# Decode holds the magnitude at a least value, GpSimd leaves the arithmetic, first pp w_in is one float32 product, w_out follows w_in

## The chip, the cores and the metric

The kernel runs on 1 core of one Trainium2 chip. Its engines are TensorE (PE in the profile, with PEld for the loads of the stationary operand), VectorE (DVE), ScalarE (ACT), GpSimd (POOL) and SyncE (SP), whose queue issues every DMA here. The metric is the device time in microseconds (us). Before the change the median of 3 runs is 1566.36 us (1564.33 to 1568.11).

## The reference, cut to what matters

```
p_packed = softmax(scale * p @ k.T) @ v            # attn1: 32 rows of p per head, 576 keys
x        = softmax(scale * q @ p_packed.T) @ p_packed   # attn2, reshaped to 4608 x 512
h = x @ w_in ;  r = maximum(h, 0)
g = s * (r * r) + b ;  x2 = g @ w_out              # 512 -> 2048 -> 512
a = x2 @ w1 ;  bb = x2 @ w2
out = ((a * bb) @ w3) @ w_out2                     # 512 -> 1024 -> 1024 -> 512
```

Batch 8, 8 heads, 576 tokens each, head width 64. All tensors are float32 in the reference; the weights reach the kernel as 64-bit floats.

## The kernel before, in words

A weight tile is loaded as 128 x 512 64-bit floats (512 KB) and turned into 32-bit floats by bit work (class `Decode`): `square` (L147, ACT) makes a mask tile `m`, `bits1` and `bits2` (L151, L157, L164, DVE) shift and join the two halves of each number, and a last step multiplies by the mask, either on DVE (L169) or in two GpSimd operations (L173, L176). `raw` holds three loads at a time, `x` three decoded tiles.

Products run as three float32r matmuls: `mm3` (L87, L90, L91) multiplies a high and a low part, which `split` makes (L80 or L82 the high part, L84 the low part, DVE or GpSimd).

The order of the work is one Python program; a scheduler turns it into one fixed order for each engine and for the DMA queue of SP. It runs in these stages:

- Start. `attn1_steps(0, ...)` computes the packed p of batches 0 and 1 (units u = 0 to 3), and beside it the 16 tiles of w_in are decoded into `winx`. Then `attn2_steps(0)` computes the attention of batch 0; beside it `W_split` and `W_tile` fold packed p into w_in: 16 products of a w_in tile (`wps`), whose results are split into `wph`, `wpl` for batch 0 and stored as `w2_d` for batch 1. After them `win_store` (L578) writes the 16 decoded tiles to DRAM.
- Steady part. 256 steps, 32 for a batch: `step_h(idx+2)` makes h (6 matmuls), `r` (ACT, L641), `g` (DVE, L643), and its two halves `gh` (ACT, L80) and `gl` (GpSimd, L84); `step_x(idx)` multiplies them by w_out tile f = idx mod 16 (12 matmuls into four banks). After each 16 steps `xst` (L675, L677) takes the result. In the first 16 steps `wo_load` and `wo_dec` load and decode one tile of w_out each. Beside the steps run: attn2 of the next batch, attn1 of the next pair of batches, the W tiles for that pair (steps 49, 113 and 177 on; w_in is loaded again and split each time), and from step 36 on `job`, which decodes the weights of the second part. The last 8 pairs of jobs (step 144 on) end in `combine`: seven sums of w1 and w2 are split into one buffer `Shl` and stored (L715).
- Second part: products with w1, w2 (`prod`), then with w3 and w_out2 (`yps`). The change touches nothing there but the name of a buffer.

Of the kernel before, what the change touches and what calls it, by code (L numbers as in the profile page):

```python
# [22 lines left out]
def fused_kernel(  # L23
# [51 lines left out]
    TINY = 1.125 * 2.0 ** -30  # L75
# [22 lines left out]
    win_d = [tc.dram_tile([P, FC], F32, name=f"win_{n}") for n in range(NFC * NPAIR)]  # L98
    x2_d = [[tc.dram_tile([DM, HS], F32, name=f"x2_{b}_{h}") for h in range(2)] for b in range(B)]
# [26 lines left out]
    RAWB, XB = 3, 3  # L126
# [4 lines left out]
    class Decode:  # L131
# [13 lines left out]
        def square(self):  # L145
            self.m = dec.tile([P, 512], BF16, tag="m", name="m", bufs=2)
            nc.scalar.activation(self.m, self.hf, AF.Square)  # L147

        def bits1(self, pin=False, out=None):
            self.x = dec.tile([P, 512], I32, tag="x", name="x", bufs=XB) if out is None else out  # L150
            ins = nc.vector.tensor_scalar(  # L151
                out=self.x, in0=self.hw, scalar1=3, scalar2=0x3FFFFFFF,
                op0=ALU.logical_shift_left, op1=ALU.bitwise_and,
            )
            if pin:
                tc.keep_in_program_order(ins)
            nc.vector.scalar_tensor_tensor(  # L157
                out=self.x, in0=self.hw, scalar=-0x40000000, in1=self.x,
                op0=ALU.bitwise_and, op1=ALU.bitwise_or,
            )  # L160

        def bits2(self, e2="v"):
            xu, xf = self.x.bitcast(U32), self.x.bitcast(F32)
# [4 lines left out]
            if e2 == "v":  # L168
                nc.vector.scalar_tensor_tensor(  # L169
                    out=xf, in0=self.m, scalar=TINY, in1=xf, op0=ALU.is_ge, op1=ALU.mult  # L170
                )
            else:
                nc.gpsimd.tensor_scalar(  # L173
                    out=self.m, in0=self.m, scalar1=TINY, scalar2=None, op0=ALU.is_ge
                )
                nc.gpsimd.tensor_tensor(out=xf, in0=self.m, in1=xf, op=ALU.mult)  # L176
            self.f = xf

    if True:
# [28 lines left out]
        def q_sc(b, t, ps):  # L208
            for pr in range(NPAIR):
                c = 64 * (pr ^ (b % 2))  # L210
                for o in range(tok(t) // SUB):
# [3 lines left out]
                        ppT[b // 2][:, pr, b % 2, :], start=True, stop=True,  # L215
# [193 lines left out]
        def D_ev(u, ps_of):  # L409
            b, g = divmod(u, NG)  # L410
            if u % 4 == 0:
                ppT[b // 2] = ppp.tile([P, NPAIR, 2, 2 * NP], F32, tag="ppT", name="ppT", bufs=2)
# [3 lines left out]
                ppT[b // 2][:, 2 * g:2 * g + 2, b % 2, :],  # L416
# [6 lines left out]
        def pp_split(bp):  # L423

            hi = stg.tile([P, NPAIR, P], F32R, tag="pph", name="pph", bufs=1)
            lo = stg.tile([P, NPAIR, P], F32R, tag="ppl", name="ppl", bufs=1)
            for o in range(2):
                for bb in range(2):
                    c = slice(64 * (bb ^ o), 64 * ((bb ^ o) + 1))
                    split(hi[:, o::2, c], lo[:, o::2, c], ppT[bp][:, o::2, bb, :])  # L430
# [44 lines left out]
        wd, wx = {}, {}  # L475

        def win_load(n):
            fc, pr = divmod(n, NPAIR)
            wd[n] = Decode(w_in[pr * P:(pr + 1) * P, fc * FC:(fc + 1) * FC])
# [4 lines left out]
        wo_t, wod = {}, {}  # L484

        def wo_load(f):
            wod[f] = Decode(w_out[f * P:(f + 1) * P, :], pin=f > 1)

        def wo_dec(f):
            d = wod.pop(f)  # L490
            d.square()
            d.bits1()
            d.bits2("g" if f % 4 == 3 else "v")
            if f >= NW // 2:
# [585 lines left out]
```

## Time and profile before

| | |
|---|---|
| median of 3 runs | 1566.36 us |
| the profiled execution | 1571.24 us, its span 1569.5 us |
| mean granted TensorE clock | 0.962 of full speed |
| busy: PE, DVE, ACT, POOL | 1467.2, 959.7, 632.5, 423.5 us |
| start, to the end of step 16 | 0 to 198.8 us |
| steps 17 to 256 | 198.8 to 955 us |
| second part | 955 to 1569.5 us |

The busy time of an engine is the union of its instructions; matmuls are pipelined, so a PE that is shown as busy may still lose time between them. The end of each 16 steps can be read from the first `xst` copy.

### The profile page before, as it was taken

How to read it: one execution, taken by the hardware profiler on the slowest of the kernel's cores; microseconds unless marked ns; L12 is line 12 of the kernel's file. 1: busy time of each engine (PE TensorE's matmuls, PEld its weight loads, DVE VectorE, ACT ScalarE, POOL GpSimd, SP SyncE). 2: the span in 40 equal slices, each digit the busy share in tenths (PEclk: the TensorE clock that was granted, in tenths of full speed). 3: DMA queues.
4: the chain of work that ended last, by engine and by line, in shares of the span. 5: the costliest groups of instructions: out<-in, count | busy, mean ns of one | idle time of the engine just before them, and what ended most of it. 6: DMA issues, size and time to landing. Idle time of an engine off the chain costs nothing.

```text
span 1569.5 us, 26929 instructions
## 1 busy us (share of the span) xinstructions
PE 1467.2 (93%) x10136; PEld 1336.9 (85%) x10136; DVE 959.7 (61%) x1913; ACT 632.5 (40%) x1465; POOL 423.5 (27%) x418
## 2 busy tenths in 40 slices
PE   6677799999999999988789999999999999999998
PEld 3356699999999889878579998899999999999996
DVE  6985844674657566756666425457665575756552
ACT  3465454565544565544555434212121131212111
POOL 6763623553334442434453331000000000000000
PEclk7578999999999999999889999999999999999999
DMA  9738532544535544533655115345656474555541
GB/s 247 208 98 232 154 103 73 158 147 128 142 108 171 161 143 138 156 120 121 201 174 169 57 46 181 109 163 206 218 193 212 164 244 162 183 196 167 202 161 41
DMA packets 142899, 245.57 MB, mean 156 GB/s; under 512 B 52144, under 2 KB 103344, under 8 KB 136624
## 3 DMA queue, kind: packets, MB, share of 16 engines
q1 hardware_dynamic: 142768, 243.84, 49.8%
q8 instruction: 80, 1.31, 0.4%
q14 instruction: 51, 0.42, 0.1%
HBM read 191.37 MB, written 52.43 MB: 155 GB/s over the span
## 4 chain that ended last, share of the span: by engine, by line
PE 71%; DMA 13%; DVE 9%; ACT 2%; issue 2%; POOL 1%; SPq 0%; ACTq 0%; DVEq 0%; POOLq 0%
PE prod L90 7%; PE prod L87 7%; PE prod L91 7%; DMA whl<-Shl 6%; PE xps L90 6%; PE xps L87 6%; PE xps L91 6%; PE yps L90 4%; PE yps L91 4%; PE yps L87 4%; PE hps L87 3%; PE hps L90 3%; PE hps L91 3%; DMA raw<-in_moe_w_out_dram 2%; DMA x<-win 1%
## 5 line engine op out<-in xcount | busy, mean ns | idle before, releaser
L84 POOL TENSOR_TENSOR gl<-g,gh 128x288 fp32r<-128x288 f32 (+1 forms) x256 | 228.3, 893 | 398.5 <-ACT gh L80 380.9
L90 PE MATMUL xps<-gl,wo 128*128 128x288 f32 (+1 forms) x1024 | 302.2, 302 | 3.8 <-POOL gl L84 3.6
L91 PE MATMUL xps<-gh,wo 128*128 128x288 f32 (+1 forms) x1024 | 298.4, 299 | 0.0
L87 PE MATMUL xps<-gh,wo 128*128 128x288 f32 (+1 forms) x1024 | 266.1, 302 | 7.4 <-POOL wo L84 5.2
L643 DVE SCALAR_TENSOR_TENSOR g<-hps,sb_s,r 128x288 f32<-128x288 f32 x256 | 130.6, 513 | 163.8 <-ACT r L641 152.4
L87 PE MATMUL prod<-xc,whl 128*128 128x384 f32 x672 | 225.8, 336 | 2.4 <-DMA whl<-whl 2.4
L90 PE MATMUL prod<-xc,whl 128*128 128x384 f32 x672 | 226.4, 337 | 0.0
L91 PE MATMUL prod<-xc,whl 128*128 128x384 f32 x672 | 225.8, 336 | 0.0
L90 PEld LDWEIGHTS xps<-gl,wo 128*128 128x128 f32 x1024 | 194.7, 190 | 10.0 <-POOL gl L84 6.8
L91 PEld LDWEIGHTS xps<-gh,wo 128*128 128x128 f32 x1024 | 194.6, 190 | 2.4 <-issue 1.4
L87 PEld LDWEIGHTS xps<-gh,wo 128*128 128x128 f32 x1024 | 180.8, 191 | 13.9 <-POOL wo L84 6.7
L87 PE MATMUL hps<-ATh,wpl 128*128 128x288 f32 x512 | 159.0, 311 | 13.0 <-DVE wpl L84 6.3
L90 PE MATMUL hps<-ATl,wph 128*128 128x288 f32 x512 | 155.3, 303 | 0.0
L91 PE MATMUL hps<-ATh,wph 128*128 128x288 f32 x512 | 154.9, 303 | 0.0
L80 ACT CAST gh<-g 128x288 fp32r<-128x288 f32 (+1 forms) x256 | 110.2, 432 | 104.6 <-DVE g L643 92.3
L641 ACT ACTIVATE r<-hps 128x288 f32<-128x288 f32 x256 | 104.3, 409 | 93.0 <-PE hps L91 91.9
L87 PEld LDWEIGHTS prod<-xc,whl 128*128 128x128 f32 x672 | 126.7, 189 | 9.8 <-issue 2.7
L90 PEld LDWEIGHTS prod<-xc,whl 128*128 128x128 f32 x672 | 126.6, 188 | 7.9
L91 PEld LDWEIGHTS prod<-xc,whl 128*128 128x128 f32 x672 | 126.7, 189 | 0.1
L87 PEld LDWEIGHTS hps<-ATh,wpl 128*128 128x128 f32 x512 | 99.0, 194 | 21.1 <-DVE wpl L84 9.3
L90 PE MATMUL yps<-w,c 128*128 128x512 f32 x288 | 113.5, 394 | 0.0
L87 PE MATMUL yps<-w,c 128*128 128x512 f32 x288 | 112.4, 391 | 0.3 <-DVE c L84 0.3
(327 smaller groups left out, 2605.9 us busy)
## 6 DMA issues: line engine op xcount, KB each, us to landing
whl<-whl SPq DMA_DIRECT2D x48, 1792.0 KB, 7.3
raw<-in_moe_w_dram SPq DMA_DIRECT2D x32, 512.0 KB, 4.6
whl<-Shl SPq DMA_DIRECT2D x56, 256.0 KB, 2.5
raw<-in_moe_w_out_dram SPq DMA_DIRECT2D x24, 512.0 KB, 4.1
x<-win SPq DMA_DIRECT2D x48, 256.0 KB, 3.0
k<-in_k_dram SPq DMA_DIRECT2D x16, 576.0 KB, 6.6
v<-in_v_dram SPq DMA_DIRECT2D x16, 576.0 KB, 6.4
q<-in_q_dram SPq DMA_DIRECT2D x72, 128.0 KB, 3.2
```

The costliest lines, as they stand in the source:

```text
L80: nc.scalar.copy(hi, src)
L84: eng.tensor_tensor(out=lo, in0=src, in1=hi.bitcast(F32), op=ALU.subtract)
L87: ins = nc.tensor.matmul(ps, wl, xh, start=start, stop=False)
L90: nc.tensor.matmul(ps, wh, xl, start=False, stop=False)
L91: nc.tensor.matmul(ps, wh, xh, start=False, stop=stop)
L641: nc.scalar.activation(r_, ps[:, :HS], AF.Relu)
L643: nc.vector.scalar_tensor_tensor(out=g[:, :HS], in0=ps[:, :HS], scalar=sb_s[:, 0:1], in1=r_, op0=ALU.mult, op1=ALU.mult)
```

## The change

- `Decode` no longer makes a mask. ACT writes the magnitude of the high word (`Abs`), DVE holds it at a least value 2^-15, then come the same three bit operations, the first of them now in place on the magnitude. No operation of it is on GpSimd.
- Low parts (`gl`, `wo`) go to DVE, and `g` becomes a square on ACT; the factor s is applied with `xst`. The sums of `combine`, one copy of p and a 2-column copy stay on GpSimd.
- The W tiles of the first pair of batches multiply packed p by w_in directly, as one float32 matmul instead of three float32r ones; no `W_split` there. Packed p lies so that the tile needs no rearranging, and `pp_split` is one split.
- One list of 32 tiles, w_in then w_out, is loaded three ahead and decoded by `dec_next`: in each step of the first attn1, in every third step of the first attn2, and in the first steps. Each `win_store` follows its W tile.
- The second pair's W tiles split w_in and store the split tile (`wsp_d`); the two later pairs load that (512 KB) instead of splitting.
- W tiles start three steps later (`WR` 20), attn1 of the later pairs starts at steps 0, 40 and 104 with units 8 or 12 steps apart, and `Shl` has two buffers.

```diff
-        def square(self):
-            self.m = dec.tile([P, 512], BF16, tag="m", name="m", bufs=2)
-            nc.scalar.activation(self.m, self.hf, AF.Square)
         def bits1(self, pin=False, out=None):
-            ins = nc.vector.tensor_scalar(
-                out=self.x, in0=self.hw, scalar1=3, scalar2=0x3FFFFFFF,
-                op0=ALU.logical_shift_left, op1=ALU.bitwise_and,
-            )
+            xi, xf = self.x.bitcast(I32), self.x.bitcast(F32)
+            ins = nc.scalar.activation(xf, self.hf, AF.Abs)
+            nc.vector.tensor_scalar_max(xf, xf, LEAST)
...
+            nc.vector.tensor_scalar(
+                out=xi, in0=xi, scalar1=3, scalar2=0x3FFFFFFF,
+                op0=ALU.logical_shift_left, op1=ALU.bitwise_and,
+            )
...
-            if e2 == "v":
-                nc.vector.scalar_tensor_tensor(
-                    out=xf, in0=self.m, scalar=TINY, in1=xf, op0=ALU.is_ge, op1=ALU.mult
-                )
-            else:
-                nc.gpsimd.tensor_scalar(
-                    out=self.m, in0=self.m, scalar1=TINY, scalar2=None, op0=ALU.is_ge
-                )
-                nc.gpsimd.tensor_tensor(out=xf, in0=self.m, in1=xf, op=ALU.mult)
-            self.f = xf
+            self.f = self.x.bitcast(F32)
...
         def W_split(k, src):
-            hi = stg.tile([P, FC], F32R, tag="sh", name="sh", bufs=2)
-            lo = stg.tile([P, FC], F32R, tag="sl", name="sl", bufs=2)
-            split(hi, lo, src, "s" if k % 2 else "v", "g")
-            sw[k] = (hi, lo)
+            t = stg.tile([P, 2, FC], F32R, tag="shl", name="shl", bufs=WB)
+            split(t[:, 0], t[:, 1], src)
+            nc.sync.dma_start(out=wsp_d[k], in_=t.bitcast(F32))
+            sw[k] = t
...
-            ph, pl = pps[bp]
-            wh, wl = sw.pop(k)
-            mm3(ps, ph[:, pr, :], pl[:, pr, :], wh, wl, True, True)
+            if bp == 0:
+                nc.tensor.matmul(
+                    ps, ppT[0][:, 2 * pr:2 * pr + 2, :].rearrange("p a c -> p (a c)"), win_at(k),
+                    start=True, stop=True,
+                )
+            else:
+                ph, pl = pps[bp]
+                t = sw.pop(k)
+                mm3(ps, ph[:, pr, :], pl[:, pr, :], t[:, 0], t[:, 1], True, True)
...
+        def dec_next():
+            n = ndec[0]
+            if n >= NW + FB1:
+                return
+            ndec[0] += 1
+            d = dq.pop(0)
+            if n < NW:
+                d.bits1(out=win_at(n).bitcast(I32))
+                d.bits2()
+            else:
+                f = n - NW
+                d.bits1()
+                d.bits2()
...
+                split(wo_t[f][:, 0, :], wo_t[f][:, 1, :], d.f)
+            dec_load()
...
+        wps_of = Banks(("a2", "h"))
         first = attn2_steps(0, Banks(("x0", "x1", "x2", "x3")))
-        wo_load(0)
-        wo_load(1)
         for i in range(len(first)):
-            if i % 2 == 0 or i > 10:
-                if nw < NW:
-                    W_split(nw, win_at(nw))
-                    W_tile(0, nw, a2_ps("wps"))
-                    nw += 1
+            if nw < NW:
+                W_tile(0, nw, wps_of("wps"))
+                nw += 1
+                win_store()
             run(first, i)
...
+            if i % 3 == 2:
+                dec_next()
...
-            nc.vector.scalar_tensor_tensor(
-                out=g[:, :HS], in0=ps[:, :HS], scalar=sb_s[:, 0:1], in1=r_, op0=ALU.mult, op1=ALU.mult
-            )
+            nc.scalar.activation(g[:, :HS], r_, AF.Square)
...
-            split(gh, gl, g[:, :n], "s", "g")
+            split(gh, gl, g[:, :n])
...
-                t = ap.tile([P, 2, h], F32R, tag="Shl", name="Shl", bufs=1)
+                t = ap.tile([P, 2, h], F32R, tag="Shl", name="Shl", bufs=2)
...
-        def W_load(k):
+        def W_load(k, first):
+            if not first:
+                sw[k] = stg.tile([P, 2, FC], F32R, tag="shl", name="shl", bufs=WB)
+                nc.sync.dma_start(out=sw[k].bitcast(F32), in_=wsp_d[k])
+                return
...
-        WR = 17
+        WR = 20
...
-        AP1 = 8
+        AT1 = {0: 1, 40: 2, 104: 3}
...
-            for d in (4, 1, 0):
+            for d in (4, WB, 1, 0):
```

Where instructions move, three places of the fixed order show it. First the DMA queue of SP about the end of the first W tiles, before (`win` are the stores of decoded w_in, `raw` the loads of w_out, k, q, v those of attention):

```order
L578 DMA win_71<-winx_189 128x512
L578 DMA win_72<-winx_189 128x512
L187 DMA q<-in_q_dram 64x8x64 x2
L134 DMA raw<-in_moe_w_out_dram 128x512 x3
L290 DMA k<-in_k_dram 96x4x384
L187 DMA q<-in_q_dram 64x8x64 x2
L297 DMA v<-in_v_dram 96x4x384
L134 DMA raw<-in_moe_w_out_dram 128x512
L290 DMA k<-in_k_dram 96x4x384
L134 DMA raw<-in_moe_w_out_dram 128x512 x6
```

The same queue now, from the sixth load of w_out on (`w_0_0` is the store of a W tile, `w2i` its load for the next batch):

```order
L136 DMA raw<-in_moe_w_out_dram 128x512 x4
L289 DMA v<-in_v_dram 96x4x384
L179 DMA q<-in_q_dram 64x8x64 x2
L453 DMA w_0_0_105<-w2o 128x512
L588 DMA win_58<-winx_198 128x512
L136 DMA raw<-in_moe_w_out_dram 128x512
L588 DMA win_59<-winx_199 128x512
L136 DMA raw<-in_moe_w_out_dram 128x512
L461 DMA w2i<-w_0_0_105 128x512
L136 DMA raw<-in_moe_w_out_dram 128x512
L588 DMA win_57<-winx_198 128x512
L453 DMA w_0_1_106<-w2o 128x512
```

The loads of w_out stood behind all stores of w_in, and now stand between them.

Second, VectorE during the decode of w_in, before:

```order
L151 TENSOR_SCALAR winx_184<-raw 128x512
L157 SCALAR_TENSOR_TENSOR winx_184<-raw,winx_184 128x512
L164 SCALAR_TENSOR_TENSOR winx_184<-raw,winx_184 128x512
L151 TENSOR_SCALAR winx_184<-raw 128x512
L157 SCALAR_TENSOR_TENSOR winx_184<-raw,winx_184 128x512
L403 TENSOR_TENSOR pvx<-pvp,rec 128x128
L164 SCALAR_TENSOR_TENSOR winx_184<-raw,winx_184 128x512
```

And now:

```order
L151 TENSOR_SCALAR winx_200<-winx_200 128x512
L154 TENSOR_SCALAR winx_200<-winx_200 128x512
L158 SCALAR_TENSOR_TENSOR winx_200<-raw,winx_200 128x512
L165 SCALAR_TENSOR_TENSOR winx_200<-raw,winx_200 128x512
L395 TENSOR_TENSOR pvx<-pvp,rec 128x128
L151 TENSOR_SCALAR winx_200<-winx_200 128x512
L154 TENSOR_SCALAR winx_200<-winx_200 128x512
L158 SCALAR_TENSOR_TENSOR winx_200<-raw,winx_200 128x512
```

A tile took three operations here and now takes four; the first two are in place.

Third, ScalarE in a `combine`, before (`Shl` is the high part of a sum, `r` and `gh` belong to the steps):

```order
L80 CAST Shl<-S 128x256
L80 CAST gh<-g 128x288
L641 ACTIVATE r<-hps 128x288
L80 CAST gh<-g 128x288
L229 ACTIVATE E_8917<-E_8917 128x256
L641 ACTIVATE r<-hps 128x288
L80 CAST Shl<-S 128x256
L80 CAST gh<-g 128x288
```

And now:

```order
L80 CAST Shl<-S 128x256
L80 CAST gh<-g 128x288
L637 ACTIVATE r<-hps 128x288
L639 ACTIVATE g<-r 128x288
L637 ACTIVATE r<-hps 128x288
L80 CAST Shl<-S 128x256
L639 ACTIVATE g<-r 128x288
L80 CAST gh<-g 128x288
L80 CAST ATh<-atp 128x2x64
L80 CAST Shl<-S 128x256
```

The square of each step (L639) has come into this queue, and the casts into `Shl` stand closer together.

## Rows read from the trace of the kernel before

**Rows 1.** Page, part 2: GB/s moved in 40 equal slices of the span.
```profile
GB/s 247 208 98 232 154 103 73 158 147 128 142 108 171 161 143 138 156 120 121 201 174 169 57 46 181 109 163 206 218 193 212 164 244 162 183 196 167 202 161 41
```

**Rows 2.** Stretches cut after steps 16, 128, 224: length, busy PE, PEld, DVE, ACT, POOL, clock, DMA.
```profile
0.00:198.80 198.80, 142.69 (x1079) 105.13 (x1080) 151.48 (x295) 102.15 (x224) 122.03 (x99) 0.79 0.67 186
198.80:527.50 328.70, 328.01 (x2879) 311.89 (x2878) 196.55 (x420) 179.63 (x431) 128.30 (x133) 1.00 0.45 130
527.50:878.00 350.50, 315.80 (x2473) 286.36 (x2472) 229.28 (x463) 192.83 (x468) 148.10 (x156) 0.96 0.50 153
```

**Rows 3.** Timeline of ACT, first xst copy after steps 16, 32, 64, 224.
```profile
198.80 0.50 ACT L675 ACTIVATE xst<-xps,xbias 128x288 f32<-128x288 f32 x1
...
243.73 0.50 ACT L675 ACTIVATE xst<-xps,xbias 128x288 f32<-128x288 f32 x1
...
336.49 0.50 ACT L675 ACTIVATE xst<-xps,xbias 128x288 f32<-128x288 f32 x1
...
878.02 0.48 ACT L675 ACTIVATE xst<-xps,xbias 128x288 f32<-128x288 f32 x1
```

**Rows 4.** Timeline of POOL: low parts of w_out tiles 5, 6 and 16.
```profile
92.54 1.26 POOL L84 TENSOR_TENSOR wo<-x,wo 128x512 fp32r<-128x512 f32 x1
148.42 1.33 POOL L84 TENSOR_TENSOR wo<-x,wo 128x512 fp32r<-128x512 f32 x1 [18.02 <-ACT wo L80]
...
194.07 1.29 POOL L84 TENSOR_TENSOR wo<-x,wo 128x512 fp32r<-128x512 f32 x1
```

**Rows 5.** Timeline of the SP queue, 131 to 142 us.
```profile
131.99 5.57 SPq L578 DMA_DIRECT2D win<-winx  x8
...
139.14 2.15 SPq L134 DMA_DIRECT2D raw<-in_moe_w_out_dram  x3
```

**Rows 6.** Instructions on tiles winx, raw, hps: ns min/median/max, first and last start.
```profile
L157 DVE SCALAR_TENSOR_TENSOR winx<-raw,winx x16: 675/902/1545, 5.4 to 61.9; 128x512 int32<-128x512 int32 x16
L164 DVE SCALAR_TENSOR_TENSOR winx<-raw,winx x16: 676/807/1642, 6.1 to 63.8; 128x512 uint32<-128x512 uint32 x16
L82 DVE CAST sh<-winx x8: 367/419/831, 8.7 to 115.9; 128x512 fp32r<-128x512 f32 x8
...
L151 DVE TENSOR_SCALAR x<-raw x56: 411/423/1531, 62.7 to 829.8; 128x512 int32<-128x512 int32 x56
...
L87 PE MATMUL hps<-ATh,wpl x512: 289/295/609, 106.8 to 949.3; 128*128 128x288 f32 x171
L641 ACT ACTIVATE r<-hps x256: 382/411/439, 109.4 to 950.0; 128x288 f32<-128x288 f32 x128
```

**Rows 7.** Groups by line and shape: busy us, mean ns, idle before.
```profile
L643 DVE SCALAR_TENSOR_TENSOR g<-hps,sb_s,r 128x288 f32<-128x288 f32 x256 | 130.6, 513 | 163.8 <-ACT r L641 152.4 <-POOL gl L84 8.5 <-POOL S L707 1.9
...
L84 DVE TENSOR_TENSOR wpl<-wps,wph 64x512 fp32r<-64x512 f32 x64 | 43.8, 685 | 17.9 <-ACT wph L80 17.2
...
L84 DVE TENSOR_TENSOR c<-x,c 128x384 fp32r<-128x384 f32 x96 | 49.8, 554 | 25.8 <-ACT c L80 25.7
...
L84 POOL TENSOR_TENSOR gl<-g,gh 128x288 fp32r<-128x288 f32 x240 | 212.7, 888 | 384.7 <-ACT gh L80 367.2 <-PE xps L91 4.3 <-PE atp L252 3.8
```

**Rows 8.** Timeline of PE about a float32 product of attn2 (scp).
```profile
256.02 0.69 PE L213 MATMUL scp<-ppT,qT 128*64 128x64 f32 x16
256.63 0.40 PE L91 MATMUL xps<-gh,wo 128*128 128x288 f32 x1
```

**Rows 9.** Waits between 640 and 800 us: total, times, longest.
```profile
ACT Shl L80 <- DMA whl<-Shl: 40.3, 28, 3.3
```

**Rows 10.** Chain that ended last, about 680 us: start, us, what.
```profile
680.22 0.41 ACT Shl L80
680.66 0.34 DVE Shl L84
681.11 2.41 DMA whl<-Shl
683.62 0.41 ACT Shl L80
```

More of the change, by code (lines that the diff above doesn't have):

```diff
@@ L98, in fused_kernel @@
     win_d = [tc.dram_tile([P, FC], F32, name=f"win_{n}") for n in range(NFC * NPAIR)]
+    wsp_d = [tc.dram_tile([P, 2, FC], F32, name=f"wsp_{n}") for n in range(NFC * NPAIR)]
     x2_d = [[tc.dram_tile([DM, HS], F32, name=f"x2_{b}_{h}") for h in range(2)] for b in range(B)]
@@ L214, in q_sc @@
                         ps[sl, c:c + 64], qT[b, t][:, pr, sl],
[L215 removed]
+                        ppT[b // 2][:, 2 * pr + (b + pr) % 2, :], start=True, stop=True,
                     )
@@ L426, in pp_split @@
             lo = stg.tile([P, NPAIR, P], F32R, tag="ppl", name="ppl", bufs=1)
[L427 to L430, printed above, removed]
+            flat = "p a c -> p (a c)"
+            split(hi.rearrange(flat), lo.rearrange(flat), ppT[bp].rearrange(flat))
             pps[bp] = (hi, lo)
@@ L473, in split_wp, with dec_load @@
             wch[b, fc] = (hi, lo)
[L475 to L479, printed above, removed]
+        dq, wx = [], {}
         def win_at(n):
             return winx[n // 2][:, n % 2, :]
[L484 to L494, printed above, removed]
-                wo_t[f] = sh.tile([P, 2, DM], F32R, tag="sh", name=f"wo{f}", bufs=NW // 2)
-            else:
-                wo_t[f] = wop.tile([P, 2, DM], F32R, name=f"wo{f}")
-            split(wo_t[f][:, 0, :], wo_t[f][:, 1, :], d.f, "s", "g")
+        wo_t = {}
+        def dec_load():
+            n = nld[0]
+            if n >= NW + FB1:
+                return
+            nld[0] += 1
+            if n < NW:
+                fc, pr = divmod(n, NPAIR)
+                dq.append(Decode(w_in[pr * P:(pr + 1) * P, fc * FC:(fc + 1) * FC]))
+            else:
+                dq.append(Decode(w_out[(n - NW) * P:(n - NW + 1) * P, :], pin=True))
+        def dec_next():
+            n = ndec[0]
+            if n >= NW + FB1:
+                return
+            ndec[0] += 1
+            d = dq.pop(0)
+            if n < NW:
+                d.bits1(out=win_at(n).bitcast(I32))
[4 more added lines that the diff above has]
+                d.bits2()
+                if f >= NW // 2:
+                    wo_t[f] = sh.tile([P, 2, DM], F32R, tag="sh", name=f"wo{f}", bufs=NW // 2)
+                else:
+                    wo_t[f] = wop.tile([P, 2, DM], F32R, name=f"wo{f}")
+                split(wo_t[f][:, 0, :], wo_t[f][:, 1, :], d.f)
+            dec_load()
+        nld, ndec = [0], [0]
         NW = NFC * NPAIR
@@ L514, in attn1_steps @@
             us = range(4 * bp, 4 * bp + 4)
-            gap = 1 if sp > 4 else 0
-            steps = [[] for _ in range(3 * sp + 10 + gap)]
+            at = (4, 5, 6, 7, 8) if sp == 4 else (5, 7, 8, 10, 12)
+            steps = [[] for _ in range(3 * sp + at[-1] + 2)]
             steps[0].append(lambda: p_tr(bp, ps_of))
@@ L557, in run @@
                     fn()
-        win_load(0)
+        dec_load()
         load_k(0)
         load_p(0)
-        win_load(1)
+        dec_load()
         load_v(0)
         load_k(1)
+        for _ in range(RAWB - 2):
+            dec_load()
         make_identity(nc, ident)
@@ L723, in job @@
             elif stage == 1:
-                dst_[n].square()
                 dst_[n].bits1(pin=True)
@@ L777, in split_wo2 @@
             elif c < 8:
-                wo2[c] = tuple(stg.tile([P, DM], F32R, tag=t, name="wo2", bufs=2) for t in ("sh", "sl"))
+                wo2[c] = of(stg, "shl", WB)
             split(*wo2[c], wo2st.pop(c), "s", "v")
```

81 lines of the change are left out of this document (32 added, 49 removed).

## The prediction

> **What bounds the kernel now.** I read the stretches first, cut after steps 16, 128 and 224 of the 256 [rows 2]. Between 198.8 and 527.5 us PE is busy 328.0 of 328.7 us at full clock: nothing that only relieves another engine can help there. From 955 us on the second part runs in code that the change leaves alone. Two stretches are not bound by PE. In the start, to 198.8 us, PE is busy 142.7 us at a granted clock of 0.79, and between 527.5 and 878 us it is busy 315.8 of 350.5 us at 0.96. So the gain, if there is one, is looked for in these two.
>
> What a step costs when PE is the bound: step 32 ends at 243.73 and step 64 at 336.49 us [rows 3], 92.76 us for 32 steps, 2.90 us a step with the attention and the W tiles that belong to it. Against that the 96 steps of the third stretch should take 96 x 2.90 = 278 us; they take 350.5, an excess of 72 us.
>
> Why the start is long: the tiles of w_out. GpSimd writes the low part of tile 5 at 92.54 us, that of tile 6 not before 148.42, that of tile 16 at 194.07 [rows 4]. Step f needs tile f, so 11 of the first 16 steps wait for these 45.7 us. The queue shows why tile 6 is late: stores of w_in run till 137.6, and only at 139.14 come three loads of w_out [rows 5], which the order places behind them.
>
> Why the third stretch is long: ACT stands at the cast into `Shl`. Between 640 and 800 us it waits 40.3 us for the store of that one buffer, 28 times [rows 9]; behind it in ACT's queue stand `r`, `gh` and the copies that PE waits for. The chain gives the period: cast at 680.22, low part, store of 2.41 us, next cast at 683.62 [rows 10], so 3.40 us a split. A combine has 7 splits, 23.8 us, and comes every 8 steps, which PE could do in 8 x 2.90 = 23.2 us: the one buffer is the bound of that stretch.
>
> **The start, part by part.** A tile of w_in costs DVE now by the medians 0.42 (the first operation, as in the row of `x`) + 0.90 + 0.81 = 2.13 us [rows 6], more where GpSimd runs beside it. It will cost two in-place operations and two joins. The trace has no in-place operation from SBUF on this shape; the nearest rows are 0.37, the shortest cast of such a tile, and 0.42, the shift from `raw` [rows 6]; the bounds are 0.37 and 0.59 (a 128 x 384 subtraction takes 0.55 [rows 7], and an operation with one source should not be slower by more than a little). I take 0.42. The joins ran in 0.68 us at their shortest and 1.64 at their longest [rows 6]. I take the short end, 0.68, since GpSimd has no work left in the start, and keep the medians as the other end. A tile then takes 2 x 0.42 + 2 x 0.68 = 2.20 us, as long as before in the medians: the 16 tiles gain nothing by count.
>
> The Trainium skill ("SBUF — State Buffer", Who interferes with whom) says that a DVE instruction with two SBUF inputs and a GpSimd instruction that reads SBUF lock each other out for a whole instruction. The spread from 0.68 to 1.64 agrees. By that rule all joins fall to the short end, by the medians alone they stay at 0.85 in the mean: 32 joins x 0.17 = 5 us of DVE.
>
> A tile of w_out costs DVE 2.20 + 0.69 for its low part (by the 64 x 512 subtraction, 685 ns [rows 7]), 46 us for 16. Before, it was a shift, two joins and a mask step on DVE, about 0.42 + 3 x 0.68 = 2.46, or 39 us, and the low part on GpSimd. W_split leaves: 8 casts of 0.42, 3 us. `g` for `gl` is even: 17 x 0.51 goes, and `gl` lies under the 0.55 of 384 columns [rows 7], say 0.46, so 1 us less. Sum on DVE: +7 - 3 - 1 = +3 us on 151.5 busy of 198.8 [rows 2], less some 10 us of contention: 140 to 155. DVE is then the busiest engine of the start and its floor.
>
> DMA floor: up to the sixteenth load of w_out the new order has 8.4 MB of w_in, 8.4 of w_out, about 9 of k, v, q, p and 6.3 of stores; 32 MB at the 247 GB/s of the first slice [rows 1] is 130 us. PE floor: the first h product stands at 106.8 us [rows 6]; all W tiles now come ahead of it and DVE does about as much up to it, so I leave it there; 16 steps x 2.90 = 46 makes 153. A product in float32 instead of three in float32r: a cluster of 16 records of 64 columns took 0.61 us [rows 8], so 512 columns in two records cost 0.3 us each if they ran alone and up to twice that if two ran side by side: 0.61 to 1.22, against three in float32r (0.295 us for 288 columns [rows 6] scales to 0.52 for 512; such records overlap, and I count a little under half of it, 0.23, for each, an estimate). I take 0.9: 16 x 0.2 = 3 us, beside DVE work, and in the range -2 to +8.
>
> I take 157 us for the end of step 16: PE's 153 and 4 for a last tile that comes late. **Term A: 198.8 - 157 = 41.8 us less**, between 20 (DVE at 155 with waits of the size that it has now) and 52 (147, contention gone and h earlier).
>
> **The third stretch.** Two buffers let two stores run at once: a split needs half of 2.41 + 0.41 + 0.43, about 1.7 us instead of 3.4 [rows 10], 12 us a combine beside 23.2 of PE. The last 16 W tiles and those of step 113 need no split (high part on DVE or ACT, low part on GpSimd). Against it: the square adds 96 x 0.41 = 39 us to ACT, by `r` [rows 6], on 193 busy of 350 [rows 2], and the three in-order pieces r, g, gh now follow each other on one queue; a late cast of `Shl` still holds them. W tiles load 512 KB each just two tiles ahead. The end cases are all of the 72 us and nothing. I take half. **Term B: 36 us less.** What is late next there: the W tiles (load, two copies on ACT, one subtraction on DVE) at the start of a batch.
>
> The page "ScalarE: Activation LUTs" of the Trainium skill (Rules for kernel authors) sends a multiply to VectorE, not ScalarE. Here the row speaks the other way: the same 288 columns took ACT 0.41 us in `r` and DVE 0.51 in `g`. By the rule the square would be the slower home and the fourth rival below would be likelier; by the rows it costs 0.1 us less a step.
>
> **At no cost or gain.** Steps 17 to 128: `gl` comes 0.43 us earlier (888 ns on GpSimd [rows 7] against 0.46), but PE is 99.8% busy there. `xst` with s: the same copies. The split and stored W tiles of step 52 on, 16 stores of 512 KB, lie beside PE-bound steps; if that cover fails, 16 x 1 us. Last steps and second part: unchanged, 0.
>
> **Sum.** 1569.5 - 41.8 - 36 = 1491.7 us of span. The profiled execution took 1571.24 us, 1.7 over its span, and 4.9 over the median 1566.36, so 1491.7 + 1.7 - 4.9 = **1489 us**. Its own range is 1472 to 1506 (term A 32 to 47, term B 26 to 48).
>
> **Rivals.** (1) Both stretches become bound by PE: start at 147 (52 less) and an excess of 15 (57 less), 1569.5 - 109 - 3.2 = 1457 us. For it: PE fills every other stretch that nothing holds. Against it: DVE's 140 to 155 us in the start. (2) SP's queue: loads of w_out still stand behind stores that wait for ACT (`w2o`), in order. If they hold them as before but for 10 us, 1569.5 - 10 - 36 - 3.2 = 1520. For it: the new queue has W-tile stores and their reloads between the loads. Against it: they are few between two loads. (3) Term B is nothing, since ACT is fuller and the 512 KB loads come late: 1569.5 - 41.8 - 3.2 = 1525. (4) Slower: ACT becomes the bound of the 240 steps after the start. r, g, gh in one queue take 0.41 + 0.41 + 0.43 us; if each step's gl comes 0.45 us later than PE can use it, 240 x 0.45 = 108, 1489 + 108 = 1597. It decides from 78 / 240 = 0.32 us a step on. Against it: h is made two steps, 5.8 us, ahead, and ACT is busy 180 of 329 us [rows 2]; with 112 x 0.41 = 46 more it has a third left. (5) The scheduler's order gives back what the tiles gain, and all stays within 0.2%: 1566.
>
> **How the numbers follow.** Forecast 49%, (1) 22, (2) 11, (3) 11, (4) 5, (5) 2. Within 0.2%, about what a measurement of this kernel can tell from no change, is 3 us. Faster: 49 + 22 + 11 + 11 = 93, less 1 for tails of (2) and (3), 92%; same 3; slower 5. The range for 8 in 10 is 1455 to 1535: it holds the forecast, (2) and (3), and the upper half of (1).
>
> **What would show it.** In the new profile the first `xst` after 16 steps should stand near 157 us, low parts of w_out should follow each other without a gap of over 10 us and end by 140, the joins on DVE should lie near 0.68 us, casts into `Shl` should wait under 15 us in all, and the stretch of steps 129 to 224 should take about 315 us. If `xst` comes after 180 term A is wrong; if ACT's wait on `Shl` goes and the stretch is still over 340 us, term B is; if steps 17 to 128 take over 335 us, the square costs.

## The result and the profile after

The changed kernel takes 1520.42 us (median of 4 runs, 1517.58 to 1521.09), the kernel before 1567.23 us in the same comparison: a ratio of 0.970, 95% interval 0.968 to 0.972, or 47 us less. The forecast was 78 us less (1489); the time lies in the range, above the forecast's own range.

The profiled execution has a span of 1519.3 us, 50.2 less than the one of before, which took 1571.24 us, 4 more than the median in the comparison: a difference of a few us in one stretch can be the execution's and not the change's. Its stretches are read first, cut at the same steps as [rows 2] (columns as there: length, busy PE, PEld, DVE, ACT, POOL with their instructions, clock, DMA share, GB/s):

```profile
0.00:173.90 173.90, 135.41 (x980) 93.73 (x980) 118.01 (x288) 96.72 (x217) 7.99 (x25) 0.78 0.75 209
173.90:522.50 348.60, 342.07 (x3076) 323.51 (x3073) 184.00 (x448) 234.43 (x569) 0.40 (x1) 0.99 0.53 158
522.50:829.30 306.80, 294.19 (x2372) 276.51 (x2372) 193.32 (x436) 217.69 (x537) 27.25 (x32) 0.98 0.61 191
```

| stretch | before | after | difference | predicted |
|---|---|---|---|---|
| start, to the end of step 16 | 198.8 | 173.9 | -24.9 | -41.8 |
| steps 17 to 128 | 328.7 | 348.6 | +19.9 | 0 |
| steps 129 to 224 | 350.5 | 306.8 | -43.7 | -36 |
| the rest | 691.5 | 690.0 | -1.5 | 0 |

The sum hides a large loss where nothing was expected. The timeline of ACT says where it lies. These are the first `xst` copies after steps 16, 32, 64, 80 and 128, as in [rows 3] (start, duration, instruction):

```profile
173.88 0.57 ACT L669 ACTIVATE xst<-xps,xbias,sb_s 128x288 f32<-128x288 f32 x1
223.09 0.59 ACT L669 ACTIVATE xst<-xps,xbias,sb_s 128x288 f32<-128x288 f32 x1
318.66 0.58 ACT L669 ACTIVATE xst<-xps,xbias,sb_s 128x288 f32<-128x288 f32 x1
382.78 0.59 ACT L669 ACTIVATE xst<-xps,xbias,sb_s 128x288 f32<-128x288 f32 x1
522.52 0.59 ACT L669 ACTIVATE xst<-xps,xbias,sb_s 128x288 f32<-128x288 f32 x1 [1.41 <-PE xps L91]
```

Steps 65 to 80 take 64.1 us (50.2 before); most other half-batches here take 43 to 49. Read in the same way, the gain of the third stretch is in steps 145 to 192, 145.0 us against 162.0, and in steps 193 to 208, 51.3 against 78.3; steps 129 to 144 stay slow (67.8 against 63.7).

The low parts of w_out tiles 5, 6, 7 and 16, now on DVE (before: [rows 4]), no longer have the gap of 56 us:

```profile
86.58 0.68 DVE L84 TENSOR_TENSOR wo<-x,wo 128x512 fp32r<-128x512 f32 x1
91.39 0.69 DVE L84 TENSOR_TENSOR wo<-x,wo 128x512 fp32r<-128x512 f32 x1 [0.74 <-ACT wo L80]
99.32 0.69 DVE L84 TENSOR_TENSOR wo<-x,wo 128x512 fp32r<-128x512 f32 x1
...
138.68 0.68 DVE L84 TENSOR_TENSOR wo<-x,wo 128x512 fp32r<-128x512 f32 x1
```

The reason stands in the DMA queue of SP, 82.5 to 90 us, where loads of w_out now stand between stores of w_in (before, [rows 5], behind all of them). This is read from the rows; no run puts the loads back:

```profile
82.50 0.42 SPq L588 DMA_DIRECT2D win<-winx  x1
83.35 0.33 SPq L136 DMA_DIRECT2D raw<-in_moe_w_out_dram  x1
83.73 0.45 SPq L588 DMA_DIRECT2D win<-winx  x1
85.42 0.33 SPq L136 DMA_DIRECT2D raw<-in_moe_w_out_dram  x1
```

The instructions of a w_in tile (ns min/median/max, first and last start; before: [rows 6]), then the first W tiles' float32 product, two records each:

```profile
L150 ACT ACTIVATE winx<-raw x16: 657/660/679, 5.0 to 60.0; 128x512 f32<-128x512 f32 x16
L151 DVE TENSOR_SCALAR winx<-winx x16: 420/427/428, 5.7 to 60.7; 128x512 f32<-128x512 f32 x16
L154 DVE TENSOR_SCALAR winx<-winx x16: 416/421/428, 6.1 to 61.6; 128x512 int32<-128x512 int32 x16
L158 DVE SCALAR_TENSOR_TENSOR winx<-raw,winx x16: 679/692/694, 6.6 to 63.5; 128x512 int32<-128x512 int32 x16
L165 DVE SCALAR_TENSOR_TENSOR winx<-raw,winx x16: 681/684/692, 7.3 to 64.6; 128x512 uint32<-128x512 uint32 x16
...
L436 PE MATMUL wps<-winx,ppT x32: 592/654/1223, 65.2 to 107.7; 128*128 128x512 f32 x32
```

The joins on DVE (L158, L165) have lost their spread: 679 to 694 ns, where they ran from 675 to 1642 beside GpSimd. The first h product comes at 118.58 us, 11.8 later than before, and PE is busy for only 80.8 of the 118.6 us until then. The windows 0 to 118.6, 118.6 to 173.9, 80 to 100 and 100 to 120 us show what each engine does:

```profile
0.00:118.60 118.60, 80.79 (x508) 44.09 (x508) 86.69 (x203) 62.35 (x127) 3.13 (x11) 0.71 0.90 250
118.60:173.90 55.30, 54.62 (x475) 49.64 (x473) 31.32 (x86) 34.38 (x90) 4.86 (x14) 0.95 0.45 121
80.00:100.00 20.00, 14.83 (x57) 6.51 (x58) 18.94 (x41) 15.65 (x29) 0.00 (x0) 0.74 1.03 312
100.00:120.00 20.00, 13.47 (x75) 7.97 (x73) 19.63 (x43) 16.03 (x33) 1.05 (x2) 0.77 0.91 304
```

From 80 to 120 us DVE is busy 38.6 of 40 us, ACT 31.7 and the DMA engines 0.97, at a granted clock about three quarters of full: three candidates for the floor (what holds the start up), which the experiments take apart. A fourth is PE itself at its lower clock level, which none of them tests. From 80 to 90 us the granted clock is 0.51 of full, the level of 1.2 GHz. There four W products (eight records) follow each other without a gap in 6.75 us, and the next one takes 1.02, at 0.98 (90 to 100 us):

```profile
84.18 6.75 PE L436 MATMUL wps<-winx,ppT 128*128 128x512 f32 x8 [0.81 <-DVE ppT L407]
...
91.20 1.02 PE L436 MATMUL wps<-winx,ppT 128*128 128x512 f32 x2
```

ACT's waits for the store of `Shl`, steps 129 to 224 (total, times, longest), first before the change and then now, are shorter by more than half, but not gone:

```profile
ACT Shl L80 <- DMA whl<-Shl: 58.1, 40, 3.3
```

```profile
ACT Shl L80 <- DMA whl<-Shl: 23.5, 20, 3.1
```

### The profile page after: what moved, and what is told of

It reads as the page before. It is cut to its first block, busy times and chain, and to the rows that moved or that the text cites. A ratio compares the mean times of both kernels' runs of the same rounds, so it can differ in the third digit from the quotient of the medians.

```text
span 1519.3 us, 26341 instructions
## 1 busy us (share of the span) xinstructions
PE 1451.3 (96%) x10120; PEld 1326.2 (87%) x10120; DVE 875.0 (58%) x1904; ACT 719.5 (47%) x1692; POOL 35.6 (2%) x58
## 4 chain that ended last, share of the span: by engine, by line
PE 84%; DMA 8%; DVE 3%; ACT 3%; issue 1%; SPq 1%; POOL 0%; ACTq 0%; DVEq 0%
PE xps L87 8%; PE xps L90 8%; PE xps L91 8%; PE prod L90 8%; PE prod L87 8%; PE prod L91 8%; PE yps L90 4%; PE yps L91 4%; PE hps L87 4%; PE yps L87 4%; PE hps L91 4%; PE hps L90 4%; DMA whl<-Shl 2%; DMA raw<-in_moe_w_in_dram 2%; PE scp L205 1%; PE s1p L337 1%
## 5 line engine op out<-in xcount | busy, mean ns | idle before, releaser
L91 PE MATMUL xps<-gh,wo 128*128 128x288 f32 (+1 forms) x1024 | 300.1, 298 | 0.0
L87 PE MATMUL xps<-gh,wo 128*128 128x288 f32 (+1 forms) x1024 | 278.3, 299 | 1.8 <-DVE ATl L84 0.7
L84 DVE TENSOR_TENSOR gl<-g,gh 128x288 fp32r<-128x288 f32 (+1 forms) x256 | 118.1, 464 | 172.8 <-ACT gh L80 171.0
L639 ACT ACTIVATE g<-r 128x288 f32<-128x288 f32 x256 | 113.1, 446 | 9.9 <-DVE gl L84 5.2
L90 PE MATMUL yps<-w,c 128*128 128x512 f32 x288 | 113.6, 395 | 0.0
L87 PE MATMUL yps<-w,c 128*128 128x512 f32 x288 | 112.6, 391 | 0.3 <-DVE c L84 0.3
L91 PE MATMUL yps<-w,c 128*128 128x512 f32 x288 | 112.8, 394 | 0.0
```

Of the source, the lines that this page charges most:

```text
L84: eng.tensor_tensor(out=lo, in0=src, in1=hi.bitcast(F32), op=ALU.subtract)
L87: ins = nc.tensor.matmul(ps, wl, xh, start=start, stop=False)
L90: nc.tensor.matmul(ps, wh, xl, start=False, stop=False)
L91: nc.tensor.matmul(ps, wh, xh, start=False, stop=stop)
L639: nc.scalar.activation(g[:, :HS], r_, AF.Square)
```

## The experiments

Where nothing else is said, an edit is made in the changed kernel (1520.4 us). Times by stretch come from the first `xst` of each run's trace, as above.

### One buffer for Shl again; two in the kernel before

```diff
-                t = ap.tile([P, 2, h], F32R, tag="Shl", name="Shl", bufs=2)
+                t = ap.tile([P, 2, h], F32R, tag="Shl", name="Shl", bufs=1)
```

> The changed kernel with one buffer for Shl. Theory (the single buffer held ACT, and with it steps 129 to 224): ACT's casts into Shl wait for the store again, 30 us or more, and steps 129 to 224 take 335 to 355 us instead of 307; total 1545 to 1570. Rival (the W tiles that come without a split, and the attention that was moved ahead, made the gain): the stretch stays under 317 us, total under 1530.

The edit in the kernel before is the reverse; to make room for it, `m` has one buffer and `xst` two.

> The kernel before with two buffers for Shl (room made by one mask buffer and two xst buffers). Theory (the buffer alone): steps 129 to 224 take 305 to 325 us instead of 350, total 1525 to 1542. Rival (the other moves of the change are needed): not under 338 us, total 1555 or more.

Measured: 1523.99 us (ratio to before 0.972, 0.969 to 0.976) with one buffer in the changed kernel, and 1553.41 us (0.991, 0.988 to 0.994) with two in the kernel before. Their steps 129 to 224, and ACT's wait for the store in them, first of the changed kernel with one buffer, then of the kernel before with two:

```profile
523.10:833.30 310.20, 297.39 (x2381) 277.94 (x2380) 185.42 (x431) 213.94 (x529) 28.15 (x32) 0.98 0.58 184
...
ACT Shl L80 <- DMA whl<-Shl: 49.7, 35, 3.5
```

```profile
528.30:861.50 333.20, 307.39 (x2479) 285.27 (x2478) 234.62 (x468) 194.26 (x470) 151.30 (x155) 0.96 0.52 161
...
ACT Shl L80 <- DMA whl<-Shl: 22.1, 19, 2.2
```

Neither came out as my theory had it. In the changed kernel ACT waits 49.7 us again and the stretch is only 3.4 us longer, no more than executions differ by; the rival's numbers hold there. In the kernel before the second buffer brings 17.3 us, nearly all in steps 145 to 192 (149.3 instead of 162.0), and nothing in 193 to 208 (77.8); its start is 4.8 us longer, and whether the smaller `m` and `xst` cost that is not shown. A wait of 50 us on ACT was real in both; only in one did it reach PE. One thing that differs beside the combines is attn1, as its second products show (L345 before, L337 after; steps 145 to 192, busy PE and its instructions):

```profile
591.20:753.20 162.00, 2.81 (x48) 0.67 (x48) 1.00 0.46 139
```

```profile
590.30:735.30 145.00, 1.38 (x16) 0.31 (x16) 1.00 0.62 191
```

Before the change attn1, whose PE work waits for ACT and DVE at each turn (`kT`, `E`), ran beside the combines, three times as many records as now. That this is the reason is argued, not shown: the low parts `gl` and `sl`, on GpSimd before and on DVE now, differ as well, and the run that moves them alone (below, with the W tiles) speaks for them.

### The attention's starts back to 64 and 128

```diff
-        AT1 = {0: 1, 40: 2, 104: 3}
+        AT1 = {0: 1, 64: 2, 128: 3}
...
-                attn1, at1 = attn1_steps(AT1[idx], 8 if idx == 0 else 12, a2_ps, a2_ps), idx
+                attn1, at1 = attn1_steps(AT1[idx], 8, a2_ps, a2_ps), idx
```

> The changed kernel with the attention of the third and fourth pair of batches starting at steps 64 and 128, its units 8 steps apart, as before the change (in the changed kernel 40 and 104, 12 apart). In the fixed order of PE the last 16 W tiles then stand from step 188 on again, as before, and not from 180 on, three between one h and the next; those of the second pair stand from 52 on and not from 55. Theory (the moved attention made both the loss at steps 65 to 80 and the gain at 193 to 208): 65 to 80 take 48 to 54 us instead of 64.1, steps 17 to 128 take 328 to 340 instead of 348.6, 193 to 208 take 68 to 80 instead of 51.3; total 1518 to 1540. Rival (the loss belongs to the W tiles' three steps' delay and to ACT's square, the gain to the decode without mask): 65 to 80 stays over 60 us, 193 to 208 under 57, total within 5 us of 1520.

Measured: 1513.76 us (0.967, 0.965 to 0.970), the lowest median here, though its interval overlaps that of the changed kernel (0.968 to 0.972). The edit sets back the starts and the spacing of the units together; which of them counts is not separated. Steps 65 to 80 take 47.1 us instead of 64.1, steps 17 to 128 331.5 instead of 348.6, steps 193 to 208 68.1 instead of 51.3. Steps 129 to 224 as a whole take 317.2, 10.4 more than in the changed kernel and 33.3 less than before. The stretch, then the half-batches 65 to 80 and 193 to 208 of this run:

```profile
504.90:822.10 317.20, 302.45 (x2486) 281.46 (x2485) 193.70 (x451) 228.97 (x556) 27.54 (x32) 0.98 0.62 195
...
316.80:363.90 47.10, 47.10 (x368) 45.31 (x367) 25.78 (x56) 36.77 (x87) 0.48 (x1) 1.00 0.69 239
...
712.00:780.10 68.10, 59.55 (x391) 53.32 (x390) 43.31 (x91) 50.03 (x120) 9.12 (x12) 0.95 0.86 275
```

and the same two half-batches of the changed kernel:

```profile
318.70:382.80 64.10, 57.57 (x451) 51.60 (x448) 37.91 (x83) 46.15 (x110) 0.00 (x0) 0.95 0.78 257
...
735.30:786.60 51.30, 49.13 (x363) 47.12 (x361) 32.26 (x67) 38.66 (x92) 6.06 (x8) 0.97 0.77 244
```

Both halves of the theory hold by stretch, though the total came out better than its range. PE has 451 records in steps 65 to 80 with the moved attention and 368 without, so a part of the loss there is work that was only moved; the rest is idle PE (64.1 - 57.6 us). The moved attention also gives the last W tiles their early place: their first product starts at 697.24 us in the changed kernel, 38 us ahead of the end of step 192; here at 703.61, 8 us ahead; before at 737.81, 15 us ahead:

```profile
697.24 0.50 PE L87 MATMUL wps<-shl,ppl 128*128 128x512 f32 x1
```

```profile
703.61 0.50 PE L87 MATMUL wps<-shl,ppl 128*128 128x512 f32 x1
```

```profile
737.81 0.47 PE L87 MATMUL wps<-sh,ppl 128*128 128x512 f32 x1 [0.20 <-DVE sh L82]
```

Steps 193 and on need these tiles, each of which goes ACT, DVE, ACT before its bank (one of two) is free again. The half-batches' times follow the number of `wps` records (48 for 16 tiles) in them: steps 193 to 208 hold 22 in the changed kernel (51.3 us), 36 with the pin moved as below (60.3), 42 here (68.1) and 39 before (78.3); steps 65 to 80 hold 33 in the changed kernel (64.1), 21 here (47.1) and 18 before (50.2). And 145 to 192, with the attention back and two `Shl` buffers, take 141.4 us: for that stretch the attention need not move. Whether it would be as short with the attention back and one buffer, no run shows.

### W tiles split anew; GpSimd's low parts to DVE in the kernel before

```diff
-            nc.sync.dma_start(out=wsp_d[k], in_=t.bitcast(F32))
...
-                    if d == (4 if nn == 1 else WB):
-                        W_load(k, nn == 1)
-                    elif d == 1 and nn == 1:
+                    if d == 4:
+                        W_load(k, True)
+                    elif d == 1:
```

> The changed kernel with every later W tile split anew (load of 256 KB, one cast on ACT, one subtraction on DVE, no stored split tile). One Shl buffer cost the changed kernel only 3 us, and two gave the kernel before 17 of its 44 us in steps 129 to 224, so something else made most of it. Theory (the split of the last 16 W tiles, which stood on GpSimd and DVE beside the combines, did it): steps 193 to 208 take 62 to 78 us instead of 51, total 1530 to 1545. Rival (GpSimd's slow low parts and DVE's contention with it did it; a split on ACT and DVE is cheap): 193 to 208 stays under 56 us, total under 1526.

```diff
-            split(hi, lo, src, "s" if k % 2 else "v", "g")
+            split(hi, lo, src, "s" if k % 2 else "v", "v")
...
-            split(gh, gl, g[:, :n], "s", "g")
+            split(gh, gl, g[:, :n], "s", "v")
```

> The kernel before with the low parts gl (240 steps) and sl (W splits) on DVE instead of GpSimd; all else, the one Shl buffer too, as before. Theory (GpSimd's low parts, 1.3 us for a W split and 0.9 for gl, and DVE's joins stretched beside them made most of the loss in steps 193 to 208): these take 52 to 62 us instead of 78.3, steps 129 to 224 take 315 to 335 instead of 350, total 1535 to 1552. Rival (the attention that was moved ahead out of that stretch made it): 193 to 208 stays over 70 us, total 1558 or more.

Measured: 1516.33 us (0.969, 0.966 to 0.973) without stored splits, steps 193 to 208 in 51.1 us: storing them brings nothing; the intervals of the two ratios overlap, so whether it costs 4 us stays open. In the kernel before, with gl and sl on DVE, 1556.22 us (0.992, 0.991 to 0.994): 129 to 224 take 339.3 us, 11 less, and 193 to 208 stay at 80.1. So GpSimd's share of that stretch is the smaller one, and none of 193 to 208. But steps 145 to 192 take 149.0 us instead of 162.0, as much less as with the second buffer, and here `Shl` has its one buffer and attn1 its old place. ACT's wait for the store is still there, 30.4 us in these steps against 36.9 before; the stretch in this run, then the wait before and in this run:

```profile
583.40:732.40 149.00, 144.40 (x1339) 134.98 (x1337) 109.38 (x270) 80.44 (x211) 15.28 (x18) 1.00 0.47 145
...
ACT Shl L80 <- DMA whl<-Shl: 36.9, 23, 3.3
...
ACT Shl L80 <- DMA whl<-Shl: 30.4, 24, 2.5
```

So in the kernel before, the wait costs PE some 13 us there only with the low parts on GpSimd beside it; taking away either is enough. The changed kernel has its low parts on DVE, which could explain without the moved attention why one buffer harms it so little.

### The place of the pin, and the square

A pin (`keep_in_program_order`) holds one instruction of each decode of the second part's weights in the order of the program; the change moved it from DVE to ACT.

```diff
-            ins = nc.scalar.activation(xf, self.hf, AF.Abs)
-            nc.vector.tensor_scalar_max(xf, xf, LEAST)
+            nc.scalar.activation(xf, self.hf, AF.Abs)
+            ins = nc.vector.tensor_scalar_max(xf, xf, LEAST)
```

> The changed kernel with the decode held in program order at DVE's first operation and not at ACT's Abs. In the changed kernel three Abs stand in a row at about steps 75 and 139, and DVE does twelve decode operations ahead of the low part that PE waits for. Theory (these rows of decodes are what steps 65 to 80 and 129 to 144 lose): the two halves take 49 to 58 us each instead of 64.1 and 67.8, total 1495 to 1510. Rival (the square makes ACT late there): both stay over 61 us, total within 4 us of 1520.

```diff
-            nc.scalar.activation(g[:, :HS], r_, AF.Square)
+            nc.vector.tensor_tensor(out=g[:, :HS], in0=ps[:, :HS], in1=r_, op=ALU.mult)
```

> The changed kernel with g as a product of hps and r on DVE again, without ACT's square. Rival (the square on ACT costs steps 17 to 128 their extra 20 us): the stretch falls from 348.6 to under 336 us and the total to under 1510. Theory (the square is covered; the extra 20 us are moved attention and rows of decodes): 344 to 353 us, total 1515 to 1530.

In the changed kernel three decodes stand in a row at 363 us, and the low part for which PE waits 1.53 us is behind them on DVE (timeline of ACT, then DVE):

```profile
363.26 1.79 ACT L150 ACTIVATE x<-raw 128x512 f32<-128x512 f32 x3
```

```profile
368.37 0.69 DVE L84 TENSOR_TENSOR wpl<-wps,wph 64x512 fp32r<-64x512 f32 x1
```

With the pin moved the row is gone: steps 65 to 80 take 59.4 us (4.7 less), but 129 to 144 the same 67.8, 193 to 208 60.3, and the total is 1524.98 us (0.973, 0.969 to 0.977). The row of decodes is a small part of the loss; I had taken the most visible wait for its cause.

With g on DVE the total is 1531.1 us (0.978, 0.974 to 0.982), steps 17 to 128 take 346.5 us, steps 129 to 144 72.8. The square on ACT does not make the loss of 17 to 128, of which at most 2 us go with it; taken back it costs 11 us in all, just over the top of the range given.

### The start: what is its floor

Four edits relieve suspects, some more than one: w_out decoded later (DVE, ACT and the loads), its low parts on GpSimd (DVE), stores of w_in later (DMA; on top of w_out later, whose two lines are taken out here too), and the magnitude on DVE (ACT); a fifth puts the three float32r products back.

```diff
-            if i % 3 == 2:
-                dec_next()
```

> The changed kernel without decoding w_out beside the first attn2: ten of its tiles come one a step in the first steps. Between 80 and 120 us DVE and ACT were both busy over 9 of 10 us and the first h product came at 118.6 us. Theory (w_out's decode stands in the way of the first W tiles): the first h product comes 8 to 14 us earlier, step 16 ends at 160 to 168 instead of 173.9, total 1506 to 1516. Rival (the loads are what is late: w_out then comes after its steps): step 16 ends at 174 to 190, total 1520 to 1536.

```diff
-                split(wo_t[f][:, 0, :], wo_t[f][:, 1, :], d.f)
+                split(wo_t[f][:, 0, :], wo_t[f][:, 1, :], d.f, "s", "g")
```

> The changed kernel with the low parts of the 16 w_out tiles on GpSimd, as before the change. It takes 16 x 0.69 = 11 us from DVE in the start and gives GpSimd 16 x 1.3. Theory (DVE is the floor of the start): first h product 4 to 9 us earlier, total 1511 to 1517. Rival 1 (ACT's copies of the W tiles are the floor): within 3 us, total 1517 to 1524. Rival 2 (DVE's joins stretch beside GpSimd): first h product later, total 1523 to 1532.

```diff
-                win_store()
+                if nw <= 4:
+                    win_store()
...
+            win_store()
+            win_store()
             dec_next()
```

> The changed kernel with ten tiles of w_out in the first steps (as in the run without decoding beside attn2), and 12 of the 16 stores of w_in there too, two a step: 3.1 MB leave the time before the first h product. Between 80 and 130 us the DMA engines were 0.91 to 1.07 busy at some 300 GB/s. Theory (the DMA engines are the floor of the start, 33 MB up to 130 us): first h product at 103 to 110 us instead of 114.6, step 16 ends at 158 to 166. Rival (DVE and ACT are): first h product within 3 us of 114.6, step 16 ends at 168 to 176.

```diff
-            ins = nc.scalar.activation(xf, self.hf, AF.Abs)
-            nc.vector.tensor_scalar_max(xf, xf, LEAST)
+            nc.vector.tensor_single_scalar(
+                out=xi, in_=self.hw, scalar=0x7FFFFFFF, op=ALU.bitwise_and,
+            )
+            ins = nc.vector.tensor_scalar_max(xf, xf, LEAST)
```

> The run with the decode held at DVE's first operation, but the magnitude made by an AND on DVE in place of ACT's Abs: ACT loses 32 x 0.46 us in the start and every wait for a load, DVE gains 32 x 0.37 to 0.42. Theory (ACT's queue, with Abs waiting for loads ahead of the W tiles' copies, is the floor of the start): first h product 4 to 10 us earlier, step 16 ends at 163 to 169 instead of 173. Rival (DVE is the floor): first h product 3 to 8 us later, step 16 ends at 176 to 182. After step 16 DVE has room: within 5 us.

```diff
-            if bp == 0:
-                nc.tensor.matmul(
-                    ps, ppT[0][:, 2 * pr:2 * pr + 2, :].rearrange("p a c -> p (a c)"), win_at(k),
-                    start=True, stop=True,
-                )
-            else:
-                ph, pl = pps[bp]
...
+            if bp == 0:
+                sw[k] = stg.tile([P, 2, FC], F32R, tag="shl", name="shl", bufs=WB)
+                split(sw[k][:, 0], sw[k][:, 1], win_at(k))
+            ph, pl = pps[bp]
...
+        pp_split(0)
```

> The changed kernel with the first 16 W tiles as three float32r products of split tiles (one cast on ACT and one subtraction on DVE more for each). Theory (ACT and DVE are full in that stretch): 16 x 0.6 on ACT and 16 x 0.69 on DVE put the first h product 8 to 16 us later, total 1528 to 1537. Rival (PE's float32 product, 1.14 us at full clock and 1.7 at half, is the cost, and three take 0.7): first h product 0 to 7 us earlier, total 1513 to 1520.

| run | first h product | end of step 16 | total |
|---|---|---|---|
| changed kernel | 118.6 | 173.9 | 1520.4 |
| w_out later | 114.6 | 170.2 | 1520.2 |
| its low parts on GpSimd | 115.9 | 168.9 | 1528.8 |
| w_out later, w_in stores later | 116.6 | 173.3 | 1525.1 |
| pin at DVE (reference for the next) | 117.2 | 173.0 | 1525.0 |
| magnitude on DVE | 112.4 | 173.3 | 1532.3 |
| three float32r products | 130.0 | 187.4 | 1533.2 |

The totals are known to 3 to 7 us to either side. The DMA engines are not the floor: with 3.1 MB of stores moved out of its way (against the run with w_out later alone) h came 2 us later than without, while the engines' busy share from 80 to 116 us is 0.67 (0.87 without). Of the engines, relieving ACT brings h 4.8 us ahead (magnitude on DVE, against the run with the same pin), relieving DVE 2.7, relieving both and the loads 4.0. The theories had expected 4 to 10, 4 to 9 and 8 to 14, so only ACT's was met, at its low end, and its end of step 16 was not; no single engine is shown to be the floor. What is left of it at the end of step 16 differs: nothing with the magnitude on DVE, 3.7 of the 4.0 us with w_out later, and 5.0 where h gained 2.7, with the low parts on GpSimd. Late w_out tiles do not explain that: the last low part comes at 138.7 us in the changed kernel, 141.4 with the magnitude on DVE, 141.7 with low parts on GpSimd and 150.5 with w_out later. What holds the 16 steps is open.

The float32 product is worth 13.5 us of the start, within what was expected: the three products want a cast on ACT and a subtraction on DVE for each tile, 16 x (0.62 + 0.69) us, where DVE is full and ACT busy some four fifths of the time. The granted clock is lower there too (0.57 from 60 to 130 us, 0.76 in the changed kernel); how much of the 13.5 us that makes is not shown.

GpSimd beside DVE can be seen again with the low parts put back. First the joins of w_out with GpSimd at work, then in the changed kernel:

```profile
L158 DVE SCALAR_TENSOR_TENSOR x<-raw,x x16: 673/684/1643, 65.5 to 139.2; 128x512 int32<-128x512 int32 x16
```

```profile
L158 DVE SCALAR_TENSOR_TENSOR x<-raw,x x16: 669/682/694, 66.3 to 134.1; 128x512 int32<-128x512 int32 x16
```

That the totals of these runs do not follow their starts lies in part in the W tiles' stretches: steps 65 to 80 took 69.6 us with w_out's low parts on GpSimd, with unchanged code there, and steps 129 to 144 took 89.7 with the magnitude on DVE, where the fixed order put 20 casts into `Shl` (2 in the changed kernel) beside all 48 `wps` records (36).

## Why the prediction came out as it did

**The total.** The time is that of the rival with SP's queue (1520), but its mechanism did not happen: low parts of w_out were done by 138.7 us, their longest gap was 8 us. The total came out from a start that gained less, a third stretch that gained more, and a loss of 20 us that was not in the sum. That these cancel to a time inside the range is in part luck.

**Term A, the start: -24.9 against -41.8, inside its bounds (20 to 52) and under its own range (32 to 47).** The step that failed is "PE floor: the first h product stands at 106.8 us ... DVE does about as much up to it, so I leave it there". DVE did: 86.7 us busy up to the first h against 84.4 in the kernel before. But all 16 W tiles now come ahead of h (10 before), each with 1.16 us of copies on ACT and 0.69 on DVE, and in the 40 us before h DVE was busy 38.6 and ACT 31.7; h came 11.8 us later. What its floor is stays open, as said above. Of the 24.9 us won, the float32 product makes 13.5; how the rest divides between the order of the loads and the work taken off GpSimd, no run shows. The 16 steps then took 55.3 us instead of 46 + 4, part of them at a granted clock of 0.78 (120 to 130 us). The smaller sizes: the tile took 2.22 us on DVE (predicted 2.20), the joins went to the short end, 0.68 to 0.69, as taken. The float32 product took 1.26 us of busy PE in the mean (20.1 us for 16) instead of 0.9, and the kernel was still faster with it. DVE's total up to step 16 fell to 118.0 us, not to 140 to 155: the stretch beside GpSimd had cost more than 10 us. Before, 76 joins and mask steps took 68.5 us there, 17 more than at 0.68 each, and 32 first operations 20.4, 7 more than at 0.42. Two bounds do not follow from what is given for them: DVE at 155 with the 47 us that it was idle before would end at 202, no gain at all, and the terms' own ranges add up to 1508 and not 1506. That the start came out inside its bounds is luck to that extent.

On that contention the Trainium skill ("SBUF — State Buffer", Who interferes with whom) says that a DVE instruction with two SBUF inputs contends with a GpSimd instruction that reads SBUF. The runs agree: joins of w_in up to 1.64 us with GpSimd at work and 0.694 at most without.

**Steps 17 to 128: +19.9 against 0.** The step that failed is "At no cost or gain": it priced `gl`, `xst` and the stores of split tiles, and left out the attention that starts at 40 and 104 instead of 64 and 128, although it stood in the change. The stretch has 197 PE records more than before (3076 against 2879), 118 of them by the moved attention (2958 without it), which lays attn1 beside the W tiles of steps 52 to 80, where both want ACT, DVE and the same kind of bank. With the old starts and spacing the stretch is 331.5 us. The square, which the prediction named as the culprit if this stretch came out long, is not it.

**Term B, steps 129 to 224: -43.7 against -36, within its range, but not for the reason given.** The step that failed is "the one buffer is the bound of that stretch". Its wait was read rightly, but a wait on ACT is not yet a loss on PE: with one buffer the changed kernel waits 49.7 us and loses 3.4, and the kernel before, with gl and sl on DVE, waits nearly as before and gains 11. In the kernel before the second buffer alone brings 17 us; some 13 us of either gain are in steps 145 to 192. That the last W tiles need no split brought nothing either: splitting them anew makes no loss. Of the 43.7 us the moved attention makes 10.4 in sum: it gives 193 to 208 some 17 of their 27 (68.1 without it; before 78.3), and the other stretches lose a part of that. The other 33.3 us come without it. What share of them the buffer, the low parts on DVE and the rest have in the changed kernel is open, and where the other 10 us of 193 to 208 come from, no run shows; the new decode, the square and the second buffer together with the rest are left. That the W tiles at the start of a batch are late next did hold as to the place: 65 to 80 and 129 to 144 are now the slowest half-batches, though with the old starts 65 to 80 are not (47.1).

**The fourth rival, ACT as the bound.** It did not come. The square takes 0.445 us on ACT (0.41 taken from `r`), the product on DVE 0.457. The page "ScalarE: Activation LUTs" of the Trainium skill (Rules for kernel authors) sends a multiply to VectorE. The measurement decides otherwise here: with the product on DVE the kernel took 11 us more.

## What to carry to other kernels

A long wait in a list of waits is a cost only if it reaches the engine that sets the time; take the wait away in both kernels before believing it, and take away what stands beside it too: here 30 us of the same wait stayed and 13 us of the loss went. When a change moves a whole stage, count the records of the bottleneck engine per stretch and ask what else wants the same engines there; here the move lost 17 us in one stretch and won 10 in the next. Undoing the single part that lost most gave the lowest median, 1513.8 us.

## What the runs showed of the hardware that was not expected

- A float32 product of 128 x 512 with a 128 x 128 stationary side is two records of 0.59 us at the least, 0.65 in the median. At a granted clock of 0.98 and more (90 to 110 us) a product took 1.02 to 1.13 us; four in a row at 0.51 (80 to 90 us) took 6.75.
- The 128 x 512 magnitude from every second word of a 64-bit tile takes ACT 0.66 us; a DVE pass with one source, in place on the same shape, 0.42.
- `xst` with a scale from a tile beside the bias takes 0.59 us in the median, 0.50 without ([rows 3]).
